# Attention bias by distance to a key, mirrored and skewed through memory, in another tile order

## The chip, the cores and the metric

The kernel runs on one core of one Trainium2 chip. The metric is the device time of one execution in microseconds (us). The engines are PE (TensorE; PEld is its weight load), DVE (VectorE), ACT (ScalarE), POOL (GpSimd) and SP (SyncE, which here only issues DMAs).

## The reference

Attention with a learned position bias, then two feed-forward blocks. 2 batches, 8 heads, 576 positions, head size 64; the bias network has 32 hidden units.

```python
scores = scale * q @ k^T                                  # per batch and head
rel   = pos[:, None] - pos[None, :]
psi   = log1p(abs(rel)) / log1p(max(pos[:, None], 1))     # query i, key j
h     = maximum(psi[..., None] @ w1 + b1, 0)              # 576 x 576 x 32
bias  = h @ w2                                            # 576 x 576 x 8 heads
attn  = softmax(scores + bias);  out = attn @ v
x = out as 1152 x 512;  x = (x @ w_a) * (x @ w_b) @ w_out # 512 -> 1536 -> 512
x = layernorm(h * softmax(h)) * g @ w_out2,  h = x @ w_in # 512 -> 1024 -> 512
```

The numerator of `psi` depends on the distance of query and key alone; its denominator on the query alone.

## The kernel before

**Bias.** Since ReLU commutes with a positive factor, `psi_i * h = max(w1 * log1p(|i-j|) + b1 * psi_i, 0)`. A table `tabs` holds `w1 * log1p(|distance|)` on 128 partitions (4 queries g by 32 hidden units, each g shifted by its own offset), for every signed distance. One bias piece T covers 16 queries: tile `it` of 128 queries, base 64*(r//4) and offset c = r%4, in four quads `qd` of 4 queries that lie 4 apart. There are 36 pieces: 8 for each of the tiles 0 to 3, and 4 for the last tile, whose 64 queries serve both batches. For a piece:
- `bias_hidden` (L342) makes four tiles `h` of 128 x 576: a window of `tabs` plus a column of `nb` (b1 times psi_i), then max with 0, on DVE (L351) or ACT (L353) as the table `HIDDEN` says ("v" or "a").
- `bias_sums` (L356) multiplies each `h` by `w2bd` (128 x 32, the quad's 4 queries by 8 heads) into `bps` in PSUM, two halves of 288 keys each; the four quads use four column groups of PE (L361).
- `bias_out` (L364) copies `bps` with a per-row scale into `st` (ACT, L371), and a DMA on SP's queue places `st` (128 rows of 16 queries by 8 heads) into the tile `bias_t[it]` of 128 queries x 8 heads x 576 keys (L373). `bias_t` has two buffers.

**Attention.** A unit is one query tile of one batch; units are (0,b0), (0,b1), (1,b0), ... and the last tile with both batches, 9 units of 8 heads, 72 steps. At step n the loop issues, in the order of the letters of `ORDER`: s `scores` of step n (PE, L388), b `biased` of step n-1 (DVE, L401: adds the bias and finds the extreme of the row), p `powers` (ACT, L408), h `shares` (POOL, L413 and L415), t `turned` (PE L423, ACT L426 or DVE L428), v `values` (PE, L452), k and l the keeping of turned inputs, o `bias_out`, u `bias_sums`, x whatever `later` has put down for the step (loads, `bias_hidden`, conversions). All engines run their queues in this order.

**Where bias work stands.** Tile 0 (T = 0 to 7) and T = 8 are made in a first loop before step 0. That loop also fills the second part of `tabs` for negative distances (`table` on `psi_l`, L505, copied by DVE at L497). The other pieces have a step n each (L546 to L555): hidden at n-2 and n-1, sums at n, out at n+1. `SECOND_T` gives n for T = 9 to 15, 16*i + 2*r for T = 16 to 31, `LAST_T` for the last four. From step 56 on weights of the first feed-forward block are loaded and prepared besides.

Of the kernel before, what the change touches and what calls it, by code (L numbers as in the profile page):

```python
# [17 lines left out]
P = 128  # L18
# [7 lines left out]
ORDER = ("kbhvioljptsxu", "kbihlospjtvxu", "kbihlospjxtvu")  # L26
# [3 lines left out]
SECOND_T = (3, 6, 8, 10, 12, 13, 14)  # L30
LAST_T = (48, 50, 52, 54)

HIDDEN = (("vvva", "vvva", "vvva", "vvva", "vvva", "vvva", "vvva", "vvvv"),
          ("vvvv", "avvv", "avav", "avvv", "avav", "avvv", "avav", "avvv"), ("vvvv", "avvv"))
# [20 lines left out]
def tile_kernel(ctx, tc, q, k, v, w1, b1, w2, w_a, w_b, w_out, w_in2, w_out2, g_ln, psi, rpsi, out):  # L55
# [14 lines left out]
    OFF = S - 4  # L70
    KD = DM // P
# [85 lines left out]
    with ExitStack() as actx:  # L157
# [7 lines left out]
        sp = actx.enter_context(tc.tile_pool(name="sp", bufs=4))  # L165
        ps_t = actx.enter_context(tc.tile_pool(name="ps_t", bufs=3, space=PSUM))
# [3 lines left out]
        tabs = ac.tile([P, UW + NG], F32, name="tabs")  # L170
        w2bd = ac.tile([P, 4 * H], F32, name="w2bd")
        rp = ac.tile([P, NG // 4], F32, name="rp")
        tb, nb = tabs[:, 0:UW], tabs[:, UW:].rearrange("p (c k) -> p c k", c=4)
        low = OFF - (S - 1 - 12)
        half = OFF - (P - 1 - 12)

        right, left, raw = (ep.tile([P, 2 * S], F32, tag="e", name=n) for n in ("psi_r", "psi_l", "raw"))
        w2r, rp_in = raw[:, 0:H], raw[:, H:H + NG // 4]
        nr_, nl_ = UW - half + 12, half - low + 12
        psi_r, w1r, b1r = (right[0:1, o:o + n] for o, n in ((0, nr_), (nr_, HID), (nr_ + HID, HID)))  # L180
        psi_l, psi_i = left[0:1, 0:nl_], left[0:1, nl_:nl_ + 4 * NG].rearrange("p (c t) -> p c t", c=4)
        warm = ac.tile([P, 1], F32, name="warm")
        nc.sync.dma_start(psi_r, psi[0:1, half - 12:UW])
# [10 lines left out]
        def table(a, n, row, at):  # L194

            ps = ps_s.tile([P, 2, 512], F32, tag="s", name=f"table_{a}")
            w = (n + 1) // 2
            for i in range(2):
                m = min(w, n - i * w)
                for g in range(4):  # L200
                    o = a + i * w - 4 * g - at
                    nc.tensor.matmul(ps[g * HID:(g + 1) * HID, i, 0:m], w1r, row[:, o:o + m], start=True, stop=True)
            return [(tb[:, a + i * w:a + min(n, (i + 1) * w)], ps[:, i, 0:min(w, n - i * w)]) for i in range(2)]

        halves_r = table(half, UW - half, psi_r, half - 12)
# [3 lines left out]
        nc.scalar.copy(*halves_r[0])  # L209
        nc.vector.tensor_copy(nb, ps_nb)  # L210
        nc.vector.tensor_copy(*halves_r[1])
# [125 lines left out]
        def place(T):  # L337

            it, r = divmod(T, P // 16)
            return it, 64 * (r // 4), r % 4  # L340

        def bias_hidden(T, quads=range(4)):  # L342

            it, r, c = place(T)
            for qd in quads:
                t0 = it * P + r + 16 * qd
                h = hp.tile([P, S], F32, tag="h", name=f"h_{T}_{qd}")
                win = tb[:, OFF - t0 - c:OFF - t0 - c + S]
                sc = nb[:, c, t0 // 16:t0 // 16 + 1]
                if HIDDEN[min(it, 2)][T % len(HIDDEN[min(it, 2)])][qd] == "v":  # L350
                    nc.vector.tensor_scalar(h, win, sc, 0.0, op0=ALU.add, op1=ALU.max)  # L351
                else:
                    nc.scalar.activation(h, win, AF.Relu, bias=sc)  # L353
                bias_w.setdefault(T, []).append(h)

        def bias_sums(T):  # L356

            bps = ps_s.tile([P, 2, 512], F32, tag="s", name=f"bps_{T}")
# [197 lines left out]
        steps = [(u, h) for u in range(len(units)) for h in range(H)]  # L556
# [408 lines left out]
```

## Time and profile before

| | us |
|---|---|
| runs, us | 551.5, 552.37, 2935.09 |
| median of the runs | 552.37 |
| profiled execution, its own time | 549.52 |
| its span, first to last instruction | 547.7 |
| granted TensorE clock over the span | 0.997 |

The profiled execution lies 2.85 us below the median of the runs, and its span 1.8 us below its own time. The loop before step 0 ends at about 25 us, the attention steps run to about 204 us, and the feed-forward blocks fill the rest.

### The profile page before, as it was taken

To read this page: it belongs to the slowest core of one execution; us is meant where nothing else is said; L and a number is where in the kernel's file an instruction comes from. 1 tells how busy PE (TensorE), PEld (TensorE's weight loads), DVE (VectorE), ACT (ScalarE), POOL (GpSimd) and SP (SyncE) were. 2 spreads that over 40 slices of the span, in tenths; PEclk is the share of its full clock that TensorE was granted. 3 is DMA by queue.
4 is the path that set the end of the run, shared out by engine and by line. 5 is a ranking of instruction groups with operands and counts; after the bars stand their busy time and mean duration, and the time that the engine had idled before them with its cause. 6 is when DMAs were issued, how large, how long until landed. Compare 5 with 4: busy or idle time off the path is not lost.

```text
span 547.7 us, 12391 instructions
## 1 busy us (share of the span) xinstructions
PE 531.1 (97%) x4868; PEld 472.2 (86%) x4868; DVE 423.8 (77%) x902; ACT 286.2 (52%) x596; POOL 160.2 (29%) x266
## 2 busy tenths in 40 slices
PE   7979999999999989999999999999999999999997
PEld 3658788888788879899999999999999988888886
DVE  5969899999996882597899898888885467656661
ACT  5769977788877662454555335431544432232221
POOL 2034345454556641222222212233223430000000
PEclk9989999999999999999999999999999999999999
DMA  4995433333266100643454344344400000000011
GB/s 96 195 216 111 98 96 78 82 73 78 70 150 180 41 1 2 194 140 130 154 154 133 127 129 145 123 121 149 120 35 2 0 1 20 20 19 20 19 26 52
DMA packets 53917, 49.32 MB, mean 90 GB/s; under 512 B 31582, under 2 KB 44131, under 8 KB 53860
## 3 DMA queue, kind: packets, MB, share of 16 engines
q1 hardware_dynamic: 53584, 48.52, 32.4%
q8 instruction: 38, 0.62, 0.5%
q14 instruction: 19, 0.16, 0.1%
q10 hardware_dynamic: 276, 0.02, 0.0%
HBM read 34.37 MB, written 2.36 MB: 67 GB/s over the span
## 4 chain that ended last, share of the span: by engine, by line
PE 86%; DVE 6%; issue 2%; DMA 2%; POOL 2%; ACT 1%; SPq 0%; POOLq 0%; ACTq 0%; DVEq 0%
PE pm L125 26%; PE po L125 14%; PE py L862 9%; PE ph L802 9%; PE px L452 6%; PE bps L361 6%; PE s L388 6%; PE pt L423 6%; DVE h L351 2%; PE pl L843 1%; POOL e L415 1%; DMA words<-in_moe_w_out_dram 1%; DVE e L401 1%; PE tp_q L281 1%; PE tp_k L281 1%
## 5 line engine op out<-in xcount | busy, mean ns | idle before, releaser
L99 POOL TENSOR_SCALAR f<-f 128x512 f32<-128x512 f32 x48 | 41.3, 860 | 139.9 <-ACT f L98 133.2
L125 PE MATMUL pm<-xhi,abh 128*128 128x384 f32 x240 | 80.2, 334 | 0.0
L125 PE MATMUL pm<-xhi,abl 128*128 128x384 f32 x240 | 80.2, 334 | 0.0
L125 PE MATMUL pm<-xlo,abh 128*128 128x384 f32 x240 | 80.2, 334 | 0.0
L415 POOL TENSOR_SCALAR e<-e,rec 128x576 f32<-128x576 f32 x72 | 57.9, 804 | 76.0 <-DVE rec L414 68.3
L408 ACT ACTIVATE e<-e,nm 128x576 f32<-128x576 f32 x72 | 55.8, 775 | 27.6 <-DVE nm L401 17.1
L351 DVE TENSOR_SCALAR h<-tabs 128x576 f32<-128x576 f32 x117 | 63.6, 583 | 0.0
L401 DVE CUSTOM_DVE_ANT_0 e<-s,bias 128x576 f32<-128x576 f32 x72 | 54.0, 749 | 4.1 <-PE s L388 3.4
L125 PE MATMUL po<-gh,oh 128*128 128x384 f32 x144 | 48.5, 337 | 0.6 <-DVE x2s L733 0.6
L125 PE MATMUL po<-gl,oh 128*128 128x384 f32 x144 | 48.4, 336 | 0.0
L125 PE MATMUL po<-gh,ol 128*128 128x384 f32 x144 | 48.4, 336 | 0.0
L361 PE MATMUL bps<-h,w2bd 128*32 128x288 f32 x576 | 46.7, 427 | 1.4 <-DVE h L351 0.9
L423 PE MATMUL pt<-ident,e 128*128 128x128 f32 x288 | 45.4, 280 | 2.3 <-POOL e L415 2.3
L388 PE MATMUL s<-kst,qhi 128*128 128x288 f32 x160 | 40.8, 336 | 5.0 <-DVE rec L414 3.1
L125 PEld LDWEIGHTS pm<-xhi,abh 128*128 128x128 f32 x240 | 45.1, 188 | 0.0
L125 PEld LDWEIGHTS pm<-xlo,abh 128*128 128x128 f32 x240 | 45.1, 188 | 0.0
L125 PEld LDWEIGHTS pm<-xhi,abl 128*128 128x128 f32 x240 | 45.1, 188 | 0.0
L107 DVE SCALAR_TENSOR_TENSOR f<-words,f 128x512 int32<-128x512 int32 x48 | 43.1, 897 | 1.6
L98 ACT ACTIVATE f<-words 128x512 f32<-128x512 f32 x48 | 32.5, 677 | 18.4 <-DMA words<-in_moe_w_a_dram 8.5
L144 ACT COPY one<-pm 128x384 f32<-128x384 f32 x36 | 17.2, 478 | 46.8 <-PE pm L125 46.8
L423 PEld LDWEIGHTS pt<-ident,e 128*128 128x128 f32 x288 | 32.4, 141 | 10.4 <-issue 5.7
L452 PE MATMUL px<-et,vsb 128*32 128x128 f32 (+1 forms) x1280 | 40.4, 263 | 0.3 <-DVE et L428 0.3
(134 smaller groups left out, 1235.0 us busy)
## 6 DMA issues: line engine op xcount, KB each, us to landing
bias<-st SPq DMA_DIRECT2D x40, 288.0 KB, 3.5
words<-in_moe_w_out_dram SPq DMA_DIRECT2D x20, 512.0 KB, 3.5
words<-in_moe_w_a_dram SPq DMA_DIRECT2D x12, 512.0 KB, 3.7
words<-in_moe_w_b_dram SPq DMA_DIRECT2D x12, 512.0 KB, 3.5
words<-in_moe_w_in_dram SPq DMA_DIRECT2D x8, 512.0 KB, 3.6
nat_q<-in_q_dram SPq DMA_DIRECT2D x16, 128.0 KB, 3.2
arena_hi<-in_k_dram SPq DMA_DIRECT2D x16, 128.0 KB, 2.6
vsb<-in_v_dram SPq DMA_DIRECT2D x16, 128.0 KB, 3.2
```

The lines of the kernel that those rows point to most:

```text
L107: nc.vector.scalar_tensor_tensor(out=b, in0=words[:, :, 0], scalar=29, in1=b, op0=ALU.logical_shift_right, op1=ALU.bitwise_or)
L125: nc.tensor.matmul(ps, w, x, start=(i == 0), stop=(i == n - 1))
L351: nc.vector.tensor_scalar(h, win, sc, 0.0, op0=ALU.add, op1=ALU.max)
L361: nc.tensor.matmul(bps[32 * qd:32 * qd + 32, a, 0:SH], w2bd, h[:, a * SH:(a + 1) * SH], start=True, stop=True)
L388: nc.tensor.matmul(ps[:, a, 0:SH], w, kst[:, b, h, a * SH:(a + 1) * SH], start=(m == 0), stop=(m == len(mm) - 1))
L401: nc.vector.tensor_tensor_reduce(out=halves(e), in0=ps[:, :, 0:SH], in1=halves(bias_t[it][:, h, :]), op0=ALU.add, op1=ALU.min, scale=1.0, ...
L408: nc.scalar.activation(e, e, AF.Exp, bias=nm, scale=-1.0, accum_out=sums[:, h:h + 1])
L415: nc.gpsimd.tensor_scalar(e, e, rec[:, h:h + 1], 1.0, op0=ALU.mult, op1=ALU.mult)
L423: nc.tensor.transpose(pt[:, c, :], e[:, j * TL + c * P:j * TL + (c + 1) * P], ident)
L452: nc.tensor.matmul(px[rows, p, cols], lhsT, rhs, start=(c == 0 and m == 0), stop=(c == NC), skip_group_check=True)
L802: nc.tensor.matmul(ph[u][:, a], x[:, kc, cols], w[:, kc, a * 512:(a + 1) * 512], start=(i == 0), stop=(i == 3 * KD - 1))
L862: nc.tensor.matmul(ps, x[:, c, :], w[:, c, cols], start=(i == 0), stop=(i == 3 * KF - 1))
```

## The change

The tiles are taken in the order 0, 2, 1, 3, 4. Tile 0 is made as before (a copy of its whole 576-key window). After it, the table is written again with one entry for each distance 0 to 575, not shifted by query (`table(S, ..., 0, ps_t, "t")`, copied half by ACT and half by DVE). For the pieces of the other tiles, with t0 the piece's first query, `h` and `bps` are made by distance only, for `d = max(t0 + 61, 576 - t0)` columns: 319 to 384 for tile 2, 381 to 448 for tile 1, 445 to 512 for tile 3, 573 to 576 for tile 4. All of `h` of tiles 2, 1 and 3 is on DVE. `bias_out` writes `st` of 636 columns in two ACT copies: 576 - t0 distances forward, and t0 + 60 distances backward in front of them. `st` goes by DMA to a buffer in the chip's memory (four buffers `bd`), and the new `bias_in`, one step later (part m of a step), reads it back with a pattern in which each query starts one element earlier than the one before it, straight into `bias_t`. `bias_sums` cuts at 512 columns in place of two halves. The pieces' steps move ahead by two (one for most of T = 9 to 15).

```diff
-ORDER = ("kbhvioljptsxu", "kbihlospjtvxu", "kbihlospjxtvu")
+ORDER = ("kbhvimoljptsxu", "kbihlmospjtvxu", "kbihlmospjxtvu")
-SECOND_T = (3, 6, 8, 10, 12, 13, 14)
-LAST_T = (48, 50, 52, 54)
+SECOND_T = (2, 4, 6, 8, 10, 12, 13)
+LAST_T = (46, 48, 50, 52)
+TILES = (0, 2, 1, 3, 4)
 HIDDEN = (("vvva", "vvva", "vvva", "vvva", "vvva", "vvva", "vvva", "vvvv"),
-          ("vvvv", "avvv", "avav", "avvv", "avav", "avvv", "avav", "avvv"), ("vvvv", "avvv"))
+          ("vvvv",), ("vvvv",), ("vvvv",), ("vvvv", "avvv"))
...
+    W = S + 60
+        dp = actx.enter_context(tc.tile_pool(name="dp", bufs=4, space=bass.MemoryType.DRAM))
...
-        def table(a, n, row, at):
+        def table(n, at, step, pool, tag):
...
+        def reach(T):
+            _, it, r, c = place(T)
+            t0 = it * P + r + c
+            return t0 + 60, S - t0
 
         def bias_hidden(T, quads=range(4)):
-            it, r, c = place(T)
+            n, it, r, c = place(T)
+            before, behind = reach(T)
             for qd in quads:
                 t0 = it * P + r + 16 * qd
-                h = hp.tile([P, S], F32, tag="h", name=f"h_{T}_{qd}")
-                win = tb[:, OFF - t0 - c:OFF - t0 - c + S]
+                a, d = (OFF - half - t0 - c, S) if n == 0 else (0, max(before + 1, behind))
+                h = hp.tile([P, S], F32, tag="h", name=f"h_{T}_{qd}")[:, 0:d]
+                win = tb[:, a:a + d]
...
             for qd, h in enumerate(bias_w[T]):
-                for a in range(2):
-                    nc.tensor.matmul(bps[32 * qd:32 * qd + 32, a, 0:SH], w2bd, h[:, a * SH:(a + 1) * SH], start=True, stop=True)
+                d = h.shape[1]
+                for a in range(0, d, 512):
+                    cols = slice(a, min(d, a + 512))
+                    nc.tensor.matmul(bps[32 * qd:32 * qd + 32, cols], w2bd, h[:, cols], start=True, stop=True)
...
-            nc.scalar.activation(st.rearrange("p (a j) -> p a j", a=2), bias_w.pop(T)[:, :, 0:SH], AF.Copy, scale=rp[:, k:k + 1])
-            for base in ((r,) if it < NC else (0, TL)):
-                nc.sync.dma_start(bias_t[it][base + c:base + 64:4], st)
+            if n == 0:
...
+                return
+            nc.scalar.activation(st[:, before:W], bps[:, 0:behind], AF.Copy, scale=rp[:, k:k + 1])
+            nc.scalar.activation(st[:, 0:before], bps[:, before:0:-1], AF.Copy, scale=rp[:, k:k + 1])
+            bias_w[T] = dp.tile([P, W], F32, tag="bd", name=f"bd_{T}")
+            nc.sync.dma_start(bias_w[T], st)
+
+        def bias_in(T):
+            bd = bias_w.pop(T)[:, :]
+            for rows in bias_rows(T):
+                nc.sync.dma_start(rows, bass.AP(bd.tensor, bd.offset + 60, [[8 * W - 4, 16], [W, 8], [1, S]]))
...
-        nc.sync.dma_start(psi_l, psi[3:4, low + 3 - 12:half + 3])
...
-            if T == N0 - 1:
-                for dst, ps in halves_l:
-                    nc.vector.tensor_copy(dst, ps)
+            if T == N0:
+                nc.scalar.copy(*halves[0])
+                nc.vector.tensor_copy(*halves[1])
...
-            if T == N0 - 2:
-                halves_l = table(low, half - low, psi_l, low - 12)
+            if T == N0 - 1:
+                halves = table(S, 12 + OFF - half, 0, ps_t, "t")
...
+        in_at[0] = [N0]
         for T in range(N0 + 1, S // 16):
             i, r = divmod(T - N0, N0)
-            n = LAST_T[r] if i == NC - 1 else 16 * i + (SECOND_T[r - 1] if i == 0 else 2 * r)
+            n = LAST_T[r] if i == NC - 1 else SECOND_T[r - 1] if i == 0 else 16 * i - 2 + 2 * r
...
             out_at.setdefault(n + 1, []).append(T)
+            in_at.setdefault(n + 2, []).append(T)
```

## Rows read from the trace of the kernel before

**Rows 1.** The profile's page: busy time by engine, and TensorE's clock by slice.

```profile
PE 531.1 (97%) x4868; PEld 472.2 (86%) x4868; DVE 423.8 (77%) x902; ACT 286.2 (52%) x596; POOL 160.2 (29%) x266
...
PEclk9989999999999999999999999999999999999999
```

**Rows 2.** Busy us by stretch: length, PE, PEld, DVE, ACT, POOL, clock, DMA share, GB/s.

```profile
24.70:37.00 12.30, 8.62 (x61) 6.15 (x62) 7.76 (x24) 7.28 (x15) 2.96 (x6) 0.86 0.91 207
37.00:72.00 35.00, 34.47 (x498) 28.24 (x498) 31.56 (x81) 31.30 (x66) 13.52 (x27) 1.00 0.53 119
72.00:110.00 38.00, 38.00 (x611) 31.76 (x614) 37.37 (x94) 30.73 (x67) 18.92 (x37) 1.00 0.34 82
110.00:147.00 37.00, 36.84 (x599) 30.91 (x592) 35.63 (x88) 29.77 (x66) 18.52 (x36) 1.00 0.33 77
163.20:203.70 40.50, 36.81 (x629) 32.75 (x629) 31.33 (x80) 25.90 (x64) 23.45 (x47) 1.00 0.27 76
```

**Rows 3.** The chain that ended last, 104 to 111 us: start, length, what.

```profile
104.85 0.44 PE tp_q L281 x4
105.29 1.13 PE bps L361 x16
106.42 1.09 PE px L452 x40
...
109.70 1.13 PE bps L361 x16
```

**Rows 4.** Groups of instructions by line: count, busy us, mean ns of one.

```profile
L351 DVE TENSOR_SCALAR h<-tabs 128x576 f32<-128x576 f32 x117 | 63.6, 583 | 0.0
L371 ACT ACTIVATE st<-bps,rp 128x576 f32<-128x576 f32 x36 | 26.7, 741 | 14.1 <-PE bps L361 11.6 <-issue 2.5
L353 ACT ACTIVATE h<-tabs 128x576 f32<-128x576 f32 x27 | 21.0, 785 | 0.0
L426 ACT COPY et<-pt 128x512 f32<-128x512 f32 x36 | 20.9, 581 | 5.1 <-PE pt L423 4.9
L144 ACT COPY one<-pm 128x384 f32<-128x384 f32 x36 | 17.2, 478 | 46.8 <-PE pm L125 46.8
L832 DVE TENSOR_SCALAR ev<-ev,small 128x1024 f32<-128x1024 f32 x9 | 7.3, 813 | 0.3
L268 DVE TENSOR_SCALAR arena_lo<-arena_hi 128x256 fp32r<-128x256 f32 x8 | 2.3, 284 | 0.0
```

**Rows 5.** Instructions of line L351 (DVE's `h`): their durations.

```profile
L351 DVE TENSOR_SCALAR h<-tabs x117: 494/511/1012, 6.3 to 159.5; 128x576 f32<-128x576 f32 x117
```

**Rows 6.** DVE's busy us by stretch, instructions of line L351 alone.

```profile
37.00:72.00 35.00, 9.69 (x19) 1.00 0.53 119
72.00:110.00 38.00, 17.08 (x28) 1.00 0.34 82
110.00:147.00 37.00, 16.57 (x28) 1.00 0.33 77
```

**Rows 7.** Timeline of DVE before step 0: start, length, what.

```profile
19.28 0.67 DVE L497 COPY tabs<-table 128x224 f32<-128x224 f32 x2
19.88 3.50 DVE L351 TENSOR_SCALAR h<-tabs 128x576 f32<-128x576 f32 x8
```

**Rows 8.** Transfers into tile `bias`, all 40: us from issue to landing.

```profile
DMA to landing us min/median/max: 3.2/3.5/5.2
```

**Rows 9.** DMA issues: KB each, median us to landing.

```profile
nat_q<-in_q_dram SPq DMA_DIRECT2D x16, 128.0 KB, 3.2
out_dram<-osb SPq DMA_DIRECT2D x7, 256.0 KB, 2.0
```

**Rows 10.** Timeline, 62 to 76 us: copies of T = 14 and 15, then `biased` of step 16.

```profile
66.40 0.74 ACT L371 ACTIVATE st<-bps,rp 128x576 f32<-128x576 f32 x1 [0.72 <-PE bps L361]
69.19 0.74 ACT L371 ACTIVATE st<-bps,rp 128x576 f32<-128x576 f32 x1 [0.58 <-PE bps L361]
73.33 0.74 DVE L401 CUSTOM_DVE_ANT_0 e<-s,bias 128x576 f32<-128x576 f32 x1
```

More of the change, by code (lines that the diff above doesn't have):

```diff
@@ L165, in tile_kernel @@
         sp = actx.enter_context(tc.tile_pool(name="sp", bufs=4))
+        dp = actx.enter_context(tc.tile_pool(name="dp", bufs=4, space=bass.MemoryType.DRAM))
         ps_t = actx.enter_context(tc.tile_pool(name="ps_t", bufs=3, space=PSUM))
         ps_x = actx.enter_context(tc.tile_pool(name="ps_x", bufs=1, space=PSUM))
-        tabs = ac.tile([P, UW + NG], F32, name="tabs")
+        half = OFF - (P - 1 - 12)
+        NX = UW - half
+        tabs = ac.tile([P, NX + NG], F32, name="tabs")
         w2bd = ac.tile([P, 4 * H], F32, name="w2bd")
         rp = ac.tile([P, NG // 4], F32, name="rp")
[L173 to L177, printed above, removed]
+        tb, nb = tabs[:, 0:NX], tabs[:, NX:].rearrange("p (c k) -> p c k", c=4)
+        logs, at_i, raw = (ep.tile([P, 2 * S], F32, tag="e", name=n) for n in ("logs", "psi_i", "raw"))
         w2r, rp_in = raw[:, 0:H], raw[:, H:H + NG // 4]
-        nr_, nl_ = UW - half + 12, half - low + 12
-        psi_r, w1r, b1r = (right[0:1, o:o + n] for o, n in ((0, nr_), (nr_, HID), (nr_ + HID, HID)))
-        psi_l, psi_i = left[0:1, 0:nl_], left[0:1, nl_:nl_ + 4 * NG].rearrange("p (c t) -> p c t", c=4)
+        psi_d, w1r, b1r = (logs[0:1, o:o + n] for o, n in ((0, NX + 12), (NX + 12, HID), (NX + 12 + HID, HID)))
+        psi_i = at_i[0:1, 0:4 * NG].rearrange("p (c t) -> p c t", c=4)
         warm = ac.tile([P, 1], F32, name="warm")
-        nc.sync.dma_start(psi_r, psi[0:1, half - 12:UW])
+        nc.sync.dma_start(psi_d, psi[0:1, half - 12:UW])
         nc.sync.dma_start(w1r, w1)
@@ L192, in tile_kernel @@
         nc.scalar.activation(warm, ident[:, 0:1], AF.Exp)
-        def table(a, n, row, at):
-            ps = ps_s.tile([P, 2, 512], F32, tag="s", name=f"table_{a}")
+        def table(n, at, step, pool, tag):
             w = (n + 1) // 2
+            halves = []
             for i in range(2):
                 m = min(w, n - i * w)
+                ps = pool.tile([P, 512], F32, tag=tag, name=f"table_{step}_{i}")
                 for g in range(4):
[L201 to L205, printed above, removed]
+                    o = at + i * w - step * g
+                    nc.tensor.matmul(ps[g * HID:(g + 1) * HID, 0:m], w1r, psi_d[:, o:o + m], start=True, stop=True)
+                halves.append((tb[:, i * w:i * w + m], ps[:, 0:m]))
+            return halves
+        halves = table(NX, 12, 4, ps_s, "s")
         ps_nb = ps_t.tile([P, 4, NG // 4], F32, tag="t", name="ps_nb")
@@ L208, in tile_kernel @@
             nc.tensor.matmul(ps_nb[g * HID:(g + 1) * HID], b1r, psi_i[:, :, g::4], start=True, stop=True)
-        nc.scalar.copy(*halves_r[0])
+        nc.scalar.copy(*halves[0])
         nc.vector.tensor_copy(nb, ps_nb)
-        nc.vector.tensor_copy(*halves_r[1])
+        nc.vector.tensor_copy(*halves[1])
         for g in range(4):
@@ L356, in bias_sums @@
         def bias_sums(T):
-            bps = ps_s.tile([P, 2, 512], F32, tag="s", name=f"bps_{T}")
+            bps = ps_s.tile([P, 2, 512], F32, tag="s", name=f"bps_{T}").rearrange("p a j -> p (a j)")
             for qd, h in enumerate(bias_w[T]):
-                for a in range(2):
-                    nc.tensor.matmul(bps[32 * qd:32 * qd + 32, a, 0:SH], w2bd, h[:, a * SH:(a + 1) * SH], start=True, stop=True)
+                d = h.shape[1]
+                for a in range(0, d, 512):
+                    cols = slice(a, min(d, a + 512))
+                    nc.tensor.matmul(bps[32 * qd:32 * qd + 32, cols], w2bd, h[:, cols], start=True, stop=True)
@@ L362, in bias_sums, with bias_rows @@
             bias_w[T] = bps
-        def bias_out(T):
-            it, r, c = place(T)
+        def bias_rows(T):
+            _, it, r, c = place(T)
             if it not in bias_t:
                 bias_t[it] = big.tile([P, H, S], F32, tag="big", name=f"bias_{it}")
-            st = stp.tile([P, S], F32, tag="st", name=f"st_{T}")
-            k = 9 * c + 2 * it + r // 64
-            nc.scalar.activation(st.rearrange("p (a j) -> p a j", a=2), bias_w.pop(T)[:, :, 0:SH], AF.Copy, scale=rp[:, k:k + 1])
-            for base in ((r,) if it < NC else (0, TL)):
-                nc.sync.dma_start(bias_t[it][base + c:base + 64:4], st)
+            return [bias_t[it][base + c:base + 64:4] for base in ((r,) if it < NC else (0, TL))]
@@ new lines, in bias_out @@
+        def bias_out(T):
+            n, it, r, c = place(T)
+            before, behind = reach(T)
+            st = stp.tile([P, W], F32, tag="st", name=f"st_{T}")
+            bps = bias_w.pop(T)
+            k = 9 * c + 2 * it + r // 64
+            if n == 0:
+                nc.scalar.activation(st[:, 0:S], bps[:, 0:S], AF.Copy, scale=rp[:, k:k + 1])
+                for rows in bias_rows(T):
+                    nc.sync.dma_start(rows, st[:, 0:S])
+                return
[3 more added lines that the diff above has]
+            nc.sync.dma_start(bias_w[T], st)
@@ L375, in tile_kernel @@
+        def bias_in(T):
+            bd = bias_w.pop(T)[:, :]
+            for rows in bias_rows(T):
+                nc.sync.dma_start(rows, bass.AP(bd.tensor, bd.offset + 60, [[8 * W - 4, 16], [W, 8], [1, S]]))
         st_ = {}
@@ L463, in inputs_low @@
             nc.vector.tensor_tensor(out=xlo, in0=px, in1=xhi.bitcast(F32), op=ALU.subtract)
-        units = [(it, [b]) for it in range(NC) for b in range(B)] + [(NC, list(range(B)))]
+        units = [(it, [b]) for it in TILES[:NC] for b in range(B)] + [(TILES[NC], list(range(B)))]
         qs = {}
-        extra, sums_at, out_at, keep_at = {}, {}, {}, {}
+        extra, sums_at, out_at, in_at, keep_at = {}, {}, {}, {}, {}
         def later(n, f, *args):
@@ L491, in tile_kernel @@
             fetch(w)
-        nc.sync.dma_start(psi_l, psi[3:4, low + 3 - 12:half + 3])
         N0 = P // 16
         for T in range(N0 + 2):
-            if T == N0 - 1:
-                for dst, ps in halves_l:
-                    nc.vector.tensor_copy(dst, ps)
+            if T == N0:
+                nc.scalar.copy(*halves[0])
+                nc.vector.tensor_copy(*halves[1])
             if T <= N0:
@@ L601, in tile_kernel @@
             for part in ORDER[(n >= TURN) + (n >= DRAIN)]:
-                if part == "o":
+                if part == "m":
+                    for T in in_at.get(n, []):
+                        bias_in(T)
+                elif part == "o":
                     for T in out_at.get(n, []):
```

6 lines of the change are left out of this document (3 added, 3 removed).

## The prediction

> **What bounds the kernel now.** First the page: over the whole span PE is busy 97% and DVE 77% [rows 1]. That is a mean over unlike stages, so the next view is busy time by stretch [rows 2]. The change touches only the time up to about 165 us. In 72 to 110 us PE is busy 38.00 of 38.00 us and DVE 37.37; in 110 to 147 us 36.84 and 35.63 of 37; in 37 to 72 us 34.47 and 31.56 of 35. So two engines stand at the limit at once, and ACT (30.73 of 38) and POOL (18.92) do not. The third view, the chain, tells which of the two sets the pace: it runs from one PE group to the next, without a gap, `bps` to `bps` in 109.70 - 105.29 = 4.41 us for two steps, and 0.44 us more in the periods that turn a `q` [rows 3]. `bps` takes 1.13 us of each [rows 3]. Before 37 us it is different: PE 8.62 of 12.3 us at a mean granted clock of 0.86 (most of it 2.4 GHz, a part 1.2), its one dip [rows 1, 2], with DMA at 0.91. After 163 us there is no bias work, and POOL and DVE waits appear; nothing of the change reaches there but its starting time.
>
> **PE: columns removed.** For T = 8 to 31 the before has 24 x 576 = 13,824 columns per quad. The new widths sum to 2,808 for tile 2 (320, 319, 319, 320, 381 to 384), 3,316 for tile 1 (445 to 448, 381 to 384) and 3,828 for tile 3 (445 to 448, 509 to 512): 9,952. Price: 1.13 us / 576 = 1.96 ns per column [rows 3]. So tile 2 saves 1,800 columns, 3.5 us; tile 1 1,292, 2.5 us; tile 3 780, 1.5 us: 7.6 us of PE in all. I take the proportional price, though the pieces also go from two to one per quad, which can only add to it. Tile 0 (512 + 64 in place of 288 + 288) and tile 4 (573 to 576) have the same columns: nothing, at most 0.1 us a piece for a narrow 64.
>
> **DVE: the same work in other pieces.** In T = 8 to 31 DVE had 78 of the 96 `h`, now it has all 96, the 18 of ACT among them. One costs, undisturbed, 284 ns at 256 columns and 813 at 1024, so 0.689 ns a column and 108 ns fixed [rows 4]; that gives 505 at 576, where the median is 511 [rows 5]. The mean is 583 [rows 4]: the rest, up to 1012 for one [rows 5], falls where POOL works at the same time. By stretch the mean of `h` is 510, 610 and 592 ns [rows 6], that is 0, 100 and 80 over the undisturbed. I keep these surcharges per instruction.
> - T = 9 to 15: from 18 x 510 = 9.2 us to 28 x 0.353 (355 columns) = 9.9: +0.7 us.
> - T = 16 to 23 (now tile 1): from 17.1 [rows 6] to 32 x (0.108 + 0.286 + 0.100) = 15.8: -1.3 us.
> - T = 24 to 31 (tile 3): from 16.6 to 32 x (0.108 + 0.330 + 0.080) = 16.6: 0.
>
> So PE would go below DVE, and what is gained is bounded by what DVE has idle. At 98.3% busy, which it reached in 72 to 110 us [rows 2], idle time left to use is 3.4 - 0.6 - 0.7 = 2.1 us in 37 to 72 us, 0 + 1.3 in 72 to 110, and 1.4 - 0.6 = 0.8 in 110 to 147. The smaller of PE's and DVE's sizes is taken in each: 2.0 (PE's for T = 9 to 15 would be 7/8 of 3.5, 3.1, and a little PE idling is there already), 1.5 (1.3, and a little more, since DVE had also to follow PE), 0.8. Sum **-4.3 us**. Bounds: -7.6 if DVE yields, -2 if the 18 more instructions (each 100 ns of surcharge, 1.8 us) collide more often with POOL.
>
> **ACT.** It loses 18 `h` at 785 ns, 14.1 us [rows 4]. Copies from PSUM cost 478 ns at 384 and 581 at 512 columns, 0.80 ns each; `st` at 576 takes 741, hence 280 ns fixed [rows 4]. Two copies with 636 columns together are 2 x 280 + 509 = 1,069 ns, +0.33 us for each of 28 pieces, 9.2 us. The net is -4.9 us, on an engine with 4 to 7 us idle in each stretch [rows 2]: nothing on the path. The backward read has no row; I take the forward price, with bounds of 0 and twice the column price (28 x 0.27 = 7.6 us of ACT, still inside its idle time; a gain is excluded, as the elements are the same). PSUM of `bps` is held 0.33 us longer; the next `scores` to use that buffer is over a microsecond away, so nothing.
>
> **Before step 0.** The two DVE copies, 0.67 us [rows 7], become one DVE copy of 288 columns, about 0.44, with the other half on ACT; T = 8 costs 4 x 0.26 in place of 4 x 0.44 (3.50 / 8) [rows 7]. That is up to -0.9 us on the DVE work that conversions of `k`, and so the first steps, stand behind. ACT's half must wait for all `h` of tile 0 and sits in ACT's queue ahead of a `st`, and DVE's `h` of T = 8 waits for it: I take **-0.6**, bounds 0 and -0.9. The `psi_l` load goes, one issue on SP; T = 8's write takes the place of its transfer, and its read back is new in a stretch where DMA is at 0.91 [rows 2]; 288 KB at 207 GB/s are 1.4 us, queued behind the loads of `v` and part of `k` and ahead of the rest of `k`. Bounds 0 and +1.4; 0 taken, since those have several steps until they are used.
>
> **The round trip.** This is the added wait. `bias_in` stands in SP's queue until the write has landed; queued behind it are the next piece's write and, in part x, loads of `q` that are wanted four steps later. The nearest rows: a write to memory of 256 KB lands in 2.0 us, a read of 128 KB in 3.2 [rows 9], `bias` itself in 3.2 to 5.2, median 3.5 [rows 8]. So out and in are 2.1 + 3.4 = 5.5 us, against 3.5 now. The pieces start two steps (4.4 us) earlier, which more than pays for that, but only one step earlier for T = 15. There the margin is nothing already: its `st` ends at 69.93, + 3.2 to 3.5 us is 73.1 to 73.4, and `biased` of step 16, the first that reads the tile, starts at 73.33 [rows 8, 10]. After the change its `st` comes where T = 14's did, 66.40 + 1.07 = 67.5, then 5.5 us, and 0.6 for an SP still busy with the piece before: 73.6 to 73.9. So step 16 is held up by about 0.5 us: **+0.5**, bounds 0 and 1.5. At the other tile changes the last piece is two steps earlier, some 1.9 us in hand. DMA's share rises from 0.33 to about 0.6 (318 KB more per 4.4 us), which covers itself.
>
> **Sum.** -4.3 - 0.6 + 0.5 = **-4.4 us**: the profiled 549.5 becomes 545.1, and the median of the runs, 2.85 us above it, 552.4 becomes **548.0** (0.8%).
>
> **Rivals.**
> - *All of PE's gain arrives.* DVE gives way because less of it stands under POOL. For it: the chain is all PE [rows 3]. Against it: DVE's 98% [rows 2]. -7.6 - 0.6 + 0.5: 544.7.
> - *DVE becomes the bound and pays more.* 96 short instructions meet POOL oftener than 78 long ones; gain 2 us: 550.4. For it: the surcharge already grows from 0 to 100 ns as POOL's share does [rows 2, 6].
> - *The round trip is late: slower.* All reads by `biased` of a tile's first head wait for its last piece, at three tile changes. The trip costs 5.5 us by the rows, but the only writes traced run with no other traffic. Each microsecond beyond it costs one at step 16, and beyond 7.4 one at steps 32 and 48 too. From 8.2 us on the gain of 4.9 us is gone (0.5 + 2.7 + 2 x 0.8); at 10 us the sum is -4.9 + 0.5 + 4.5 + 2 x 2.6 = +5.3: 557.7. Against it: reads under load land in 3.2 to 3.5.
> - *Odd widths run at half rate on DVE.* Half of the new widths are odd, and no row shows one. 12 of the 24 pieces x 4 x 415 columns x 0.69 ns more are 13.7 us of DVE; less 0.6 net above and the 3.6 us idle that it can use, +9.5 us: 561.8.
>
> On the third: the Trainium skill, DMA: Bandwidth & Descriptors, section Latency and other measured facts, gives memory access as 0.2 us on average and 2 us at high load. By that the trip would be some 3.6 us longer, an estimate from that page, and the third rival would hold, near 555; rows of loaded reads so far speak against. On the fourth: the page VectorE: DVE Perf Modes, section Mode 2×_2P, keeps the double rate for an odd length if source and destination are equally long, as here; no run shows it yet.
>
> **How the numbers follow.** Forecast (546 to 550) 0.55; all of PE's gain 0.13; DVE dearer 0.15; late trip 0.12; odd widths 0.05. The range leaves out about one in ten on each side: 544 to 555. A change of 2% is 11 us, about what a measurement of this kernel tells from no change. The gain is bounded by 7.6 + 0.9 us, so faster by that only if the clock's dip before 37 us goes as well: 0.02. Slower by that needs a trip of 12 us, or the half rate and more: 0.04.
>
> **What would show it.** `bps` of T = 8 to 31 should be 8 instructions a piece, of 319 to 512 columns, and 0.6 to 1.0 us on the chain. `h` on DVE at 107 + 0.69 ns a column, odd and even alike. Two-step periods of about 4.2 us, with DVE's `h` or `biased` now on the chain between PE's groups. A wait of DVE for a transfer at step 16 of at most 1.5 us, and none at 32 and 48. The stretch after the bias work should keep its length. Wrong would be: a trip over 8.2 us, ACT's backward copies far dearer, or DVE at 100% in periods of 4.4 us.

## The result and the profile after

| | before | after |
|---|---|---|
| median of the runs, us | 552.51 | 556.57 (555.67 to 558.85, 4 runs) |
| ratio, with its 95% interval | 1 | 1.0089 [1.0066, 1.0112] |
| profiled execution, own time and span, us | 549.52, 547.7 | 555.67, 553.5 |
| granted clock over the span | 0.997 | 0.990 |

The run of 2935.09 us among those before is left out of the ratio. The forecast was 548.0, in 544 to 555. The kernel became 0.9% slower, a difference clear of noise, though under 2%; the time lies above the range.

The page of the changed kernel, to be held against [rows 1]. PE lost 192 instructions, as forecast, but only 1.6 us of busy time; the dip of the clock, now to 0.7, is in the slice of 28 to 42 us. (The experiment e10 below, with the same instructions at a granted clock of 1.00, has PE busy for 525.1 us, 6.0 less than before.)

```profile
PE 529.5 (96%) x4676; PEld 465.6 (84%) x4676; DVE 421.2 (76%) x919; ACT 280.8 (51%) x607; POOL 157.9 (29%) x266
...
PEclk9979999999999999999999999999999999999999
...
bias<-bd SPq DMA_DIRECT2D x32, 288.0 KB, 3.9
bd<-st SPq DMA_DIRECT2D x28, 318.0 KB, 4.1
```

To find where the time went, the steps are the ruler: `biased` runs once per step on DVE (L436 here, L401 before), so its start in DVE's timeline, step by step, dates the whole pipeline. The table has these starts in us, for kernels of which some are explained below.

| step | before | after | difference | trip only (e2) | no trip (e1) | read later (e6) | e10 |
|---|---|---|---|---|---|---|---|
| 0 | 29.52 | 30.19 | +0.67 | 30.14 | 30.20 | 30.14 | 29.59 |
| 12 | 63.49 | 63.84 | +0.35 | 65.26 | 65.07 | 65.29 | 63.24 |
| 15 | 71.34 | 72.30 | +0.96 | | | | |
| 16 | 73.33 | 79.23 | +5.90 | 79.36 | 74.67 | 74.51 | 72.91 |
| 20 | 82.97 | 90.40 | +7.43 | 91.90 | 83.98 | 83.82 | 81.57 |
| 48 | 148.58 | 155.72 | +7.14 | 160.17 | 149.65 | 149.49 | 146.56 |
| 56 | 167.31 | 172.90 | +5.59 | 177.36 | 166.83 | 166.65 | 163.72 |
| 71 | 203.53 | 209.02 | +5.49 | 213.47 | 203.09 | 203.93 | 200.75 |

The difference column is the whole story of the profiled run. It goes up by 4.9 us in one step (15 to 16), by 1.5 more in the next four, hardly moves from 20 to 48, most of the stretch where 2.3 us were to be gained, falls by 1.55 from 48 to 56, and then stays (the spans differ by 5.8). The two profiled executions differ by 6.15 us in their own time and the medians by 4.06, so some 2 us of these differences can belong to the single executions.

What happens at step 16 stands in the timeline of DVE, ACT and SP's queue of the changed kernel (start, length, what; in brackets the idle time before and what ended it).

```profile
66.53 0.53 SPq L402 DMA_DIRECT2D bd<-st  x1
67.57 0.47 ACT L399 ACTIVATE st<-bps,rp 128x253 f32<-128x253 f32 x1 [0.70 <-PE bps L377]
67.94 0.58 ACT L400 ACTIVATE st<-bps,rp 128x383 f32<-128x383 f32 x1
70.36 0.56 SPq L408 DMA_DIRECT2D bias<-bd  x1
71.01 0.81 SPq L402 DMA_DIRECT2D bd<-st  x1
74.70 0.54 SPq L408 DMA_DIRECT2D bias<-bd  x1
79.23 0.76 DVE L436 CUSTOM_DVE_ANT_0 e<-s,bias 128x576 f32<-128x576 f32 x1 [4.37 <-DMA bd<-st]
```

The two ACT lines are the copies of T = 15: its `st` is complete at 68.52. Its write is issued only at 71.01, because the read back of T = 14 stands before it in SP's queue, and that one stood still until the write of 66.53 had landed. So the last piece needs 2.5 us for its turn in the queue, 3.7 to land, 4.5 from its read back to `biased`: 10.7 us, where the trip was put at 5.5 + 0.6. (The bracket on the last line names the write of T = 16, issued at 75.33. `biased` does not read that; it reads the tile `bias`, whose last piece is the read back of 74.70, and by the trace this one landed at 78.51.)

The waits of SP's queue in 24 to 75 us of the changed kernel say the same of all early pieces (total us, times, longest):

```profile
SPq L408 <- DMA bd<-st: 18.4, 7, 2.9
```

And the chain that ended last, in 40 to 80 us, is no longer PE's: the landing of `bd` has 50.0% of that stretch, and 9.3% more is the landing of a load of `v` that stands behind a read back in the same queue. These are two of its pieces (start, length, what):

```profile
42.88 3.90 DMA bd<-st
...
71.01 3.67 DMA bd<-st
```

Busy time by stretch, in the columns of [rows 2], shows the traffic of the trip and what the stall drags along. In 37 to 72 us the DMA share is 0.71 for the earlier 0.53. After the stall the granted clock is 0.81 in 79 to 88 us, part of it at 1.2 GHz: PE had stood idle behind `biased`. Steps 16 to 20 take 11.17 us here, 9.64 before and 9.31 in e6, where there is no stall: this much comes with it.

```profile
24.70:37.00 12.30, 10.13 (x60) 8.11 (x61) 8.80 (x28) 7.78 (x17) 2.27 (x5) 0.73 0.95 214
37.00:72.00 35.00, 31.67 (x444) 24.62 (x444) 32.53 (x92) 26.89 (x64) 13.22 (x27) 1.00 0.71 170
79.00:88.00 9.00, 6.63 (x73) 5.32 (x74) 6.16 (x18) 5.43 (x13) 3.72 (x7) 0.81 0.50 142
90.00:118.00 28.00, 27.40 (x422) 21.96 (x424) 26.07 (x73) 22.13 (x54) 13.30 (x27) 1.00 0.52 149
118.00:155.70 37.70, 37.34 (x558) 28.73 (x549) 36.60 (x94) 29.70 (x72) 18.34 (x36) 1.00 0.53 148
```

### The profile page after: what moved, and what is told of

It reads as the page before. It is cut to its first block, busy times and chain, and to the rows that moved or that the text cites. A ratio compares the mean times of both kernels' runs of the same rounds, so it can differ in the third digit from the quotient of the medians.

```text
span 553.5 us, 12090 instructions
## 1 busy us (share of the span) xinstructions
PE 529.5 (96%) x4676; PEld 465.6 (84%) x4676; DVE 421.2 (76%) x919; ACT 280.8 (51%) x607; POOL 157.9 (29%) x266
## 4 chain that ended last, share of the span: by engine, by line
PE 78%; DVE 8%; DMA 6%; issue 3%; POOL 2%; ACT 2%; SPq 1%; DVEq 0%; POOLq 0%; ACTq 0%
PE pm L128 25%; PE po L128 11%; PE py L901 9%; PE ph L841 9%; PE bps L377 5%; PE s L423 5%; PE pt L458 5%; PE px L487 4%; DMA bd<-st 4%; DVE e L436 2%; POOL e L450 2%; PE pl L882 1%; PE tp_q L287 1%; DMA words<-in_moe_w_out_dram 1%; PE tp_k L287 1%
## 5 line engine op out<-in xcount | busy, mean ns | idle before, releaser
L436 DVE CUSTOM_DVE_ANT_0 e<-s,bias 128x576 f32<-128x576 f32 x72 | 53.8, 748 | 12.5 <-PE s L423 8.1
L365 DVE TENSOR_SCALAR h<-tabs 128x576 f32<-128x576 f32 (+17 forms) x135 | 61.8, 504 | 1.0 <-ACT tabs L530 0.8
L458 PE MATMUL pt<-ident,e 128*128 128x128 f32 x288 | 46.9, 286 | 6.0 <-POOL e L450 5.8
L487 PEld LDWEIGHTS px<-et,vsb 128*32 128x32 f32 x1280 | 33.6, 110 | 13.3 <-issue 8.3
```

What stands on the lines that cost most here:

```text
L436: nc.vector.tensor_tensor_reduce(out=halves(e), in0=ps[:, :, 0:SH], in1=halves(bias_t[it][:, h, :]), op0=ALU.add, op1=ALU.min, scale=1.0, ...
L458: nc.tensor.transpose(pt[:, c, :], e[:, j * TL + c * P:j * TL + (c + 1) * P], ident)
L487: nc.tensor.matmul(px[rows, p, cols], lhsT, rhs, start=(c == 0 and m == 0), stop=(c == NC), skip_group_check=True)
```

## The experiments

Theory A: the in-order queue of SP makes the trip longer than its two transfers. Rival B: the trip is harmless in itself, and DVE, with all of `h`, pays more (the second rival of the prediction). Each ratio below is to the kernel before, timed beside it.

**e1: the change without its round trip.** `st` goes straight to `bias_t`; columns, tile order and steps stay.

```diff
-            bias_w[T] = dp.tile([P, W], F32, tag="bd", name=f"bd_{T}")
-            nc.sync.dma_start(bias_w[T], st)
+            for rows in bias_rows(T):
+                nc.sync.dma_start(rows, st[:, 60:W])
...
-            in_at.setdefault(n + 2, []).append(T)
```

> The changed kernel without the round trip: st goes straight into the bias tile, as before the change, so the skew is left out and all 16 queries of a piece get the bias of one. Columns, DVE, ACT and steps stay as changed. Theory A (the round trip is what costs): the DVE idle time of 4.4 us at step 16 and the slower clock behind it go, 6 to 7 us in all, and the time is 549 to 551 us, somewhat faster than before. Theory B (the reduced and moved work itself costs, for example 18 more h on DVE and hidden work ahead of the first biased): the time stays within 2 us of the changed kernel, above 554.

549.95 us, ratio 0.9978 [0.9964, 0.9992]. The stall is gone, with no idle time before `biased` of step 16:

```profile
74.67 0.74 DVE L436 CUSTOM_DVE_ANT_0 e<-s,bias 128x576 f32<-128x576 f32 x1
```

**e2: the round trip alone.** The kernel before, with its full columns, halves and `HIDDEN`, but written to `bd` and read back by the steps of the change.

```diff
...
+            if it > 0:
+                bias_w[T] = dp.tile([P, S], F32, tag="bd", name=f"bd_{T}")
+                nc.sync.dma_start(bias_w[T], st)
+                return
...
+                nc.sync.dma_start(bias_t[it][base + c:base + 64:4], bd)
```

> The kernel before with the round trip alone: full 576 columns, the ACT share of h and the single table as before, but st written to memory and read back one step later, and the pieces' steps moved ahead as in the change. Theory A: step 16 waits 5 us or more, as in the changed kernel, and the total is 557 to 561 us (the changed kernel's loss without its small savings). Theory B: within 2 us of before, 551 to 554.

558.78 us, 1.0130 [1.0113, 1.0147], with the same stall at the same place though not one `h` is changed:

```profile
79.36 0.76 DVE L414 CUSTOM_DVE_ANT_0 e<-s,bias 128x576 f32<-128x576 f32 x1 [3.83 <-DMA bd<-st]
```

e1 and e2 separate the two halves of the change: the trip makes it slower, the rest slightly faster. (Both also have the new steps of the pieces; what these cost is told under "Where DVE stands on the chain".) What they do not tell is whether the trip is too long or only begun too late.

**e3: the pieces earlier.**

```diff
-SECOND_T = (2, 4, 6, 8, 10, 12, 13)
+SECOND_T = (2, 4, 5, 7, 9, 10, 11)
```

> The changed kernel with T = 11 to 15 one or two steps earlier (T = 15 at step 11 in place of 13). Theory A with the latency of the trip alone as cause: two steps are about 5 us, the wait at step 16 falls from 4.4 to under 1 us, total 550 to 552. Theory A with SP's queue as cause (each piece holds the queue until its write has landed, 4.1 us, so pieces one step apart pile up): three pieces still stand one or two steps apart, so 1 to 3 us of the wait stay, total 552 to 554. Theory B: no gain, or a loss from DVE work pressed into fewer steps, 555 to 558.

556.05 us, 1.0093 [1.0078, 1.0108]: nothing won. By its time alone this is what theory B had named, and the 552 to 554 of the queue were missed; the trace tells which it is. The last piece's sums stand two steps earlier, about 4.4 us, and `biased` of step 16 starts 0.46 us earlier, at 78.77. SP's queue of e3, and ACT's copy that completes the `st` of T = 15, show why:

```profile
60.60 0.45 SPq L402 DMA_DIRECT2D bd<-st  x1
63.24 0.61 ACT L400 ACTIVATE st<-bps,rp 128x383 f32<-128x383 f32 x1
65.29 0.56 SPq L408 DMA_DIRECT2D bias<-bd  x1
65.95 0.53 SPq L402 DMA_DIRECT2D bd<-st  x1
69.79 0.55 SPq L408 DMA_DIRECT2D bias<-bd  x1
70.43 1.38 SPq L402 DMA_DIRECT2D bd<-st  x1
74.31 0.54 SPq L408 DMA_DIRECT2D bias<-bd  x1
...
78.77 0.76 DVE L436 CUSTOM_DVE_ANT_0 e<-s,bias 128x576 f32<-128x576 f32 x1 [4.31 <-issue]
```

Write, wait, read, write, wait, read: the writes follow each other at 5.35 and 4.48 us, whatever the steps say. The queue passes one piece per landing and issue, while the steps bring one in 4.4 us and the last ones 2.2 us apart, so an earlier start is used up before the last piece: its `st` is complete at 63.85, 4.7 us sooner than in the changed kernel, but its write is issued at 70.43, after 6.6 us in the queue in place of 2.5. (The profile names no releaser for DVE's 4.31 us; from the issue of the last read back, at 74.31, to `biased` it is 4.46 us, in the changed kernel 4.53.)

**e4: the writes on ACT's queue.**

```diff
-            nc.sync.dma_start(bias_w[T], st)
+            nc.scalar.dma_start(bias_w[T], st)
```

> The changed kernel with the write to memory issued on ACT's queue in place of SP's, so that it starts right behind the copy and not behind the read back of the piece before. Theory A with SP's queue as cause: T = 15's write, which stood 2.5 us in the queue, starts at once; the wait at step 16 falls by 2 to 3 us, total 552 to 554. Latency alone: unchanged wait, 556. ACT pays the issue, some 0.4 to 0.6 us for each of 28 pieces, from idle time; if that shows, up to 3 us are lost elsewhere.

555.4 us, 1.0078 [1.0039, 1.0116]: not distinguishable from the changed kernel, and short of the 552 to 554 that the queue as cause had named. The profiled execution is the slowest of five, 559.68 us, so it shows how the others can lose time, not how much. In it the stall moved. At step 16 DVE waits for nothing, but it comes there only at 82.45: the reads still hold SP, and behind one of them stand loads of `v` (`vtl`, issued at 65.84). PE waits for these in `values`, the scores stand behind that in PE's queue, and DVE waits for them at step 13:

```profile
70.18 0.64 PE L487 MATMUL px<-ett,vtl 128*32 128x128 f32 x4 [1.48 <-DMA vtl<-in_v_dram]
...
72.87 0.76 DVE L436 CUSTOM_DVE_ANT_0 e<-s,bias 128x576 f32<-128x576 f32 x1 [3.37 <-PE s L423]
```

**e5: e3, with the read back one step later for the tile that is pressed.** The read is asked for two steps after the write, when that has all but landed, and of the last pieces the next write stands ahead of it.

```diff
-            in_at.setdefault(n + 2, []).append(T)
+            in_at.setdefault(n + (3 if i == 0 else 2), []).append(T)
```

> The changed kernel with T = 11 to 15 earlier as in e3_early, and for T = 9 to 15 the read back two steps behind the write in place of one, so that the write has landed when SP comes to the read and SP's queue doesn't stand. Theory SP queue (e3_early gained nothing because each piece still held the queue some 4 us, 4.7 us with its issues): SP no longer waits 3 to 4 us for bd at every piece of the first 16 steps, the wait at step 16 goes, the clock does not dip behind it, and the total is 550 to 552 us. Rival (memory itself is slow, the transfers are the bound whatever their order): the wait stays over 3 us, 555 to 557.

550.31 us, 0.9977 [0.9962, 0.9991], 1.2% below e3's ratio. A read that is asked for *later* makes the whole faster: the write lands hardly sooner (3.6 us for e3's 3.9), but SP's queue waits 7.3 us for landings, where e3's waits 17.4. Whether the later read would do without e3's earlier pieces was not run. The same line of SP's waits, 24 to 75 us, and the start of `biased` at step 16, which now waits for nothing:

```profile
SPq L408 <- DMA bd<-st: 7.3, 5, 2.9
...
75.86 0.74 DVE L436 CUSTOM_DVE_ANT_0 e<-s,bias 128x576 f32<-128x576 f32 x1
```

**e6: e5, with T = 9 a step later**, `SECOND_T = (3, 4, 5, 7, 9, 10, 11)`, so that its `h` do not stand ahead of `biased` of step 0 on DVE.

> e5_late_in with T = 9 one step later (step 3, as before the change), so that its first two h no longer stand on DVE ahead of the first biased. If that is why the first biased came 0.7 us later than before: 0.5 to 0.7 us faster than e5_late_in; if something else held it: no difference.

550.01 us, 0.9983 [0.9968, 0.9999]: no difference from e5, and step 0 still begins at 30.14. The two `h` did cost something all the same. In the changed kernel they stand between `qlo`, the low part of a `q`, and the first `biased`, whose starts lie 1.19 us apart (29.00 and 30.19); in e6 they lie 0.74 apart (29.40 and 30.14). But `qlo` itself comes 0.40 us later, behind a wait for the second table of 1.13 us in place of 0.85 (see e11).

**e7: e1, with ACT's share of `h` given back** (tile 2 as tile 1 was before, tiles 1 and 3 every second piece).

```diff
-          ("vvvv",), ("vvvv",), ("vvvv",), ("vvvv", "avvv"))
+          ("vvvv", "avvv", "avav", "avvv", "avav", "avvv", "avav", "avvv"), ("vvvv", "avvv"), ("vvvv", "avvv"), ("vvvv", "avvv"))
```

> e1_direct (no round trip, the skew left out) with the ACT share of h put back as before the change: 10 of tile 2's 32, 4 each of tile 1's and 3's. Theory DVE (PE's saved columns gave nothing between steps 16 and 48 because DVE, with all h on it, became the bound): 2 to 3.5 us faster than e1_direct, 546.5 to 548. Rival (the chain through POOL and PE's own order sets the pace there): within 1 us of e1_direct.

548.69 us, 0.9951 [0.9936, 0.9965], 1.3 us below e1, between the two expectations. In the steps that matter little of it is to be seen: 20 to 48 take 65.38 us, e1 65.67, before 65.61. DVE had less to do there and the steps hardly got shorter, so its mean load is not what sets their pace.

**e8: e6 and that `HIDDEN` together.**

> The changed kernel, complete and with nothing left out, with all three: read back two steps behind the write for T = 9 to 15, T = 9 at step 3 and T = 11 to 15 earlier, and the ACT share of h put back. If SP's queue and DVE are the two causes and add up: 546.5 to 549.5 us, faster than before by 0.3 to 0.8%. If only the queue is: 550 to 552.

549.18 us, 0.9965 [0.9948, 0.9982]: the time is one that was named for two causes that add up, but the intervals of e6 and e8 overlap, so it does not show that.

**Where DVE stands on the chain.** The chain of the changed kernel gave the next experiment. For two pieces it goes from PE group to PE group, then DVE and POOL take over for 5 us:

```profile
94.21 0.78 PE bps L377 x8
...
98.27 0.78 PE bps L377 x8
...
103.00 0.78 PE bps L377 x8
...
106.03 0.66 DVE e L436
...
107.37 0.68 DVE et L463
108.06 0.07 DVE h L365
...
108.33 0.45 DVE h L365
108.78 0.66 DVE e L436
...
109.63 1.15 POOL e L450
...
112.56 0.89 PE bps L377 x8
```

At every eighth step DVE has, besides `biased` and `h`, a copy of `et` and the low part of the attention output (`xlo`) to make; the next `biased` comes late, POOL's `e` after it takes 1.15 us in place of its mean of 0.79, and PE waits. A mean of 93 to 97% hides that.

That both `h` of this step are on DVE comes from the pieces' new steps. In the kernel before, the piece made there is T = 15, 19, 23, 27 or 31, with its first `h` on ACT; moved ahead, it is T = 16, 20, 24, 28 or 32, with none. e2 shows the price with columns and `HIDDEN` as before: its steps 20 to 48 take 68.27 us for 65.61. The trip is not the reason, since e1 without it and e6 with it take the same 65.67 there. The `h` behind `xlo`, in the kernel before and in e2:

```profile
101.20 0.51 DVE L351 TENSOR_SCALAR h<-tabs 128x576 f32<-128x576 f32 x1
...
110.31 0.94 DVE L352 TENSOR_SCALAR h<-tabs 128x576 f32<-128x576 f32 x2
```

**e9: e7, with two `h` of just that piece on ACT**, and none of the other pieces of tiles 1 and 3.

```diff
-          ("vvvv", "avvv", "avav", "avvv", "avav", "avvv", "avav", "avvv"), ("vvvv", "avvv"), ("vvvv", "avvv"), ("vvvv", "avvv"))
+          ("vvvv", "avvv", "avav", "avvv", "avav", "avvv", "avav", "avvv"), ("aavv", "vvvv", "vvvv", "vvvv"), ("aavv", "vvvv", "vvvv", "vvvv"), ("vvvv", "avvv"))
```

> e7_direct_act (no round trip, the skew left out) with the same number of ACT h in the second and third tile, 4 each, but in other places: both quads that are made in the step where DVE also keeps the attention output (xlo, every eighth step) on ACT, for T = 16, 20, 24, 28, in place of one quad of every second piece. Theory peak (PE's saved columns give nothing from step 16 to 48 because once in eight steps DVE has biased, xlo, the copy of et, two h and biased in a row, and PE waits for that row): steps 20 to 48, 65.4 us in e7_direct_act and 65.6 before, fall to 63 to 64, and the total is 546.5 to 547.5. Rival (DVE's or POOL's total is the bound): steps 20 to 48 stay within 0.5 us, total 548 to 549.

547.04 us, 0.9910 [0.9895, 0.9925], clearly below e7, with as many `h` on ACT per four pieces as in e7, where they are those of T = 17, 19 and so on, none in the eighth step. Steps 16 to 20 take 8.65 us in place of 9.32, and 20 to 48 64.99 in place of 65.38. The total is the one that theory peak named; the 0.39 us of steps 20 to 48 lie within the 0.5 of the rival, and 63 to 64 us were not reached. Over steps 16 to 48 the same move of `h` gives e10 (below) 73.65 us for e8's 75.26, so that the place of the DVE work, more than its amount, held back part of PE's gain.

**e10: e8 with the `HIDDEN` of e9, and both copies of the second table on DVE** (below). It computes all that the changed kernel does.

```diff
-                nc.scalar.copy(*halves[0])
-                nc.vector.tensor_copy(*halves[1])
+                for dst, ps in halves:
+                    nc.vector.tensor_copy(dst, ps)
```

> e8_all, complete and with nothing left out, with the same places for ACT's h as e9_direct_peak, and both copies of the second table on DVE. Theories peak and copies together: 546 to 548 us, 0.7 to 1% faster than before. If neither holds: as e8_all, 549 to 550.

547.61 us, 0.9927 [0.9907, 0.9946]: 4.5 us below the kernel before and 1.6% below the change as made, with the round trip in it. In its chain, DVE's part at the eighth step has shrunk to `e` and `et`, with no `h` and no POOL behind them, and the four steps from `bps` to `bps` take 103.42 - 94.40 = 9.02 us in place of 112.56 - 103.00 = 9.56:

```profile
94.40 0.78 PE bps L377 x8
...
97.42 0.68 DVE e L436
...
98.76 0.70 DVE et L463
...
103.42 0.88 PE bps L377 x8
```

**e11: e6 with both table copies on DVE.** DVE's and ACT's timeline of the changed kernel before step 0:

```profile
21.29 0.46 DVE L531 COPY tabs<-table 128x288 f32<-128x288 f32 x1
21.53 0.74 ACT L395 ACTIVATE st<-bps,rp 128x576 f32<-128x576 f32 x1 [1.54 <-PE bps L377]
22.17 0.39 ACT L530 COPY tabs<-table 128x288 f32<-128x288 f32 x1
22.59 1.27 DVE L365 TENSOR_SCALAR h<-tabs 128x320 f32<-128x320 f32 x4 [0.85 <-ACT tabs L530]
```

ACT's half of the table stands behind a `st` in ACT's queue, and DVE waits 0.85 us for it ahead of T = 8.

> e6_late_in_t9 with both halves of the second table copied by DVE, in place of one by ACT. Theory: ACT's half waits in ACT's queue behind a copy of bps, so that DVE stands 1.1 us before T = 8; with both on DVE that wait goes for one more copy of 0.46 us, the first biased comes 0.6 to 0.7 us earlier, and the total falls by 0.3 to 0.7 us. Rival (the loads on SP's queue set the first steps anyway): no change.

550.29 us, 0.9969 [0.9957, 0.9981], beside e6's 0.9983 [0.9968, 0.9999]: unclear in the total. Step 0 begins at 29.46, 0.68 us earlier, and e10, with the same copies, at 29.59, where all kernels with ACT's half begin it at 30.06 to 31.42. So this wait, with the two `h` of T = 9, explains the late start; but step 16 begins at 74.47, as in e6 (74.51). The gain is lost again in between, in a stretch where steps 0 to 12 took 33.4 to 36.8 us among these kernels. What sets that length stays open.

**e12: the buffer's rows 640 elements apart in place of 636**, to see if the pitch makes the write slow.

```diff
-            bias_w[T] = dp.tile([P, W], F32, tag="bd", name=f"bd_{T}")
+            bias_w[T] = dp.tile([P, 640], F32, tag="bd", name=f"bd_{T}")
...
```

> The changed kernel with rows of the buffer in memory 640 elements (2560 bytes) apart in place of 636 (2544), the same data in them. The write lands in 4.1 us (median) in the changed kernel and in 3.1 in e2_trip_only, whose rows are 2304 bytes. If where the rows start in memory is what makes that difference: the write's median falls to about 3.1, SP is held 1 us less by each piece, the wait at step 16 shrinks by 1 to 2 us, and the total is 553 to 555 us. If it is the 10% more bytes, the load, or nothing but the places of the writes in time: 4.0 us, and 556 to 557.

555.8 us, 1.0068 [1.0042, 1.0095], overlapping with the change. Its write lands in 3.7 us (median), but e5, e6 and e10 have 3.6 to 3.8 with the old pitch: no effect of the pitch is seen.

## Why the prediction was wrong, step by step

**The round trip: the step that failed.** It was put at +0.5, bounds 0 and 1.5; the stall at step 16 is 4.9 us, and 1.5 more go in the four steps behind it, in part at the lower clock. Two things were wrong in it. One is the two transfers: the landing of the write was taken from `osb`, 2.0 us with nothing else on the way [rows 9]; here its median is 4.1. For T = 15 the write took 1.6 us more than the 2.1 that were put, and the read back, up to `biased`, 1.1 more than the 3.4. The other is the queue: the sum added the durations of *one* piece and put "0.6 for an SP still busy with the piece before", where it was 2.5, 1.9 more. (Another 1.0 us was there already when the `st` of T = 15 was complete, at 68.52 for 67.5.) The paragraph did say that the next piece's write is queued behind the read that waits, but did not price that. A queue that waits for each landing passes one piece per 4.5 to 5.4 us (e3), while the steps bring one in 4.4, the last two 2.2 apart. So it was false too that the earlier start "more than pays for that", since the delay of each piece is handed to the next. (Of T = 9 to 15 the pieces 9, 14 and 15 were moved by one step, the other four by two.) e1 (no trip, no stall), e2 (trip alone, stall), e3 (earlier, no gain) and e5 (read later, no stall) show it together. The third rival ended near the result, at 557.7, with the right first place and sign; its point of decision, 8.2 us, was passed with 10.7. That its number is so near is in part luck: it spoke of three tile changes and took the gain of 4.9 us to be there. Only the first change stalled, at 32 and 48 DVE has no wait for a transfer, as forecast, and most of the gain did not come.

The Trainium skill, DMA: Bandwidth & Descriptors, section Latency and other measured facts, gives 2 us for a memory access at high load against 0.2 on average; the write here took 2.1 us more than in the quiet (4.1 for 2.0, with 318 KB for 256), which is the direction and about the size of that rule. "rows of loaded reads so far speak against" gave too much weight to reads: the median of the read back is 3.9 us, close to the 3.4 taken, and that of the write is not close to 2.1. The queue's 1.9 us come on top of this.

**PE's columns and the bound by DVE: the second step that failed, on the gain's side.** The price per column was right: `bps` is 8 instructions and 0.78 us at 381 to 384 columns, 0.89 at 445 to 448 on the chain, against 1.13 for 576. But the sum let the gain through up to a busy share of 98.3%, -1.5 and -0.8 us for T = 16 to 23 and 24 to 31. e1, free of the trip, needs 74.98 us for steps 16 to 48 of these pieces, the kernel before 75.25: 0.3 us of the 2.3 arrived. A stretch that is 95% busy on average had one place per eight steps where DVE was full, and PE waited there. The new steps of the pieces, which the sum took only as a gain for the trip, had brought a second `h` on DVE to that place; with the old columns this costs 2.7 us over steps 20 to 48 (e2). e9 and e10 need 73.64 and 73.65 us for steps 16 to 48, so that 1.6 us of the gain arrive with two `h` per four pieces on ACT. Why not more is open. Steps 0 to 15 (-2.0 forecast) took 0.3 us longer than before; e1 has no gain there either (41.99 us, before 41.82); why is open.

**DVE pays more** (second rival): it had to be told apart from the bound above, and e7 does so: with less load on average, but in other steps, 0.3 us of steps 20 to 48 go.

**Before step 0:** -0.6 was forecast, +0.67 came. The sum left out the two `h` of T = 9 that now stand on DVE ahead of the first `biased`: from the start of `qlo` to that of `biased` it is 1.19 us, before 0.77. The text named ACT's half "ahead of a `st`"; the trace has it behind the `st` of T = 6, and the wait of 0.85 us on DVE was left out of the sum too. Without both (e11) step 0 begins 0.06 us before that of the kernel before, so another 0.5 of the forecast is missing. The clock does not tell why: in 24.7 to 37 us it is 0.73 in e11 and 1.00 in e10, which begins step 0 later, at 29.59.

**Not forecast:** steps 48 to 56 became 1.55 us shorter (17.18 for 18.73). e2, with full columns, has 17.19, and e1, without the trip, 17.18. What both share with the change is the new steps of the pieces, so it comes from these; that it is the distance from the last tile's work is argued, not shown.

**Right:** odd widths. In the groups by form, `h` on DVE costs no more for 319 and 445 columns than for 320 and 448 (446 and 447, even and odd, have higher means, 536 and 546 ns), which ends the fourth rival and agrees with the rule of VectorE: DVE Perf Modes, section Mode 2×_2P, of the Trainium skill, that was set beside it. The backward copy costs what the forward one does (447 columns, one instruction of each):

```profile
L365 DVE TENSOR_SCALAR h<-tabs 128x448 f32<-128x448 f32 x8 | 3.5, 482 | 0.0
...
L365 DVE TENSOR_SCALAR h<-tabs 128x445 f32<-128x445 f32 x8 | 3.2, 447 | 0.0
...
L365 DVE TENSOR_SCALAR h<-tabs 128x320 f32<-128x320 f32 x8 | 2.8, 397 | 0.8 <-ACT tabs L530 0.8
L365 DVE TENSOR_SCALAR h<-tabs 128x319 f32<-128x319 f32 x8 | 2.7, 378 | 0.0
...
L399 ACT ACTIVATE st<-bps,rp 128x447 f32<-128x447 f32 x1 | 0.6, 635 | 0.2 <-PE bps L377 0.2
...
L400 ACT ACTIVATE st<-bps,rp 128x447 f32<-128x447 f32 x1 | 0.6, 629 | 0.0
```

## What to carry to other kernels

A wait for a landed transfer on an in-order queue is priced as a rate, not a delay: work out how often the queue can pass a piece with the wait in it, compare that with how often pieces come, and put the read back late enough that the landing is over, or behind the next write. Before a gain on one engine is bounded by the mean idle time of another, follow the chain through a whole period of the schedule, here eight steps, and find the one place where the other engine is full; two instructions moved away from there did more than as many moved elsewhere. And when pieces of work are shifted in time, see which of them now meets that place.

## What the runs showed of the hardware

- Landing of a write to memory of about 300 KB: 2.0 us in the quiet (256 KB), a median of 4.1 at a DMA share of 0.5 to 0.7.
- After PE's idle time at step 16 the granted clock was 0.81 over 79 to 88 us, and steps 16 to 20 took 1.5 us more than before: this stall cost more than its own length.
- Reads back that wait for their write in SP's queue let one piece pass per 4.5 to 5.4 us (e3); asked for one step later they no longer held up step 16 (550.31 us for 556.05).
- Reading PSUM backward costs ACT the same as forward (629 and 635 ns at 447 columns), and odd widths cost DVE nothing (378 and 447 ns at 319 and 445 columns, 397 and 482 at 320 and 448).
